# w2's seventh rows fetched mid-run in transfers of three rows, and the rest of w2 in four parts

## The chip, the cores and the metric

One core of a Trainium2 chip runs the whole kernel. The metric is device time in microseconds (us), as the median of timed executions; the kernel before takes 1312.24 us (three runs, 1311.43 to 1312.91).

## The reference

One decoding step for eight tokens (batch 8, model width 512). The normalised input goes into two branches, whose results are added to the input:

```python
xn = layernorm(x)                              # 8 x 512
q = xn @ wq                                    # 32 heads of 128; 8 key/value heads
p = softmax(q k^T * 128**-0.5)                 # 8192 cached keys for each head
a = (p @ v) @ wo                               # wo: 4096 x 512
h = xn @ w1 + b1                               # 1792 wide
m = (h * tanh(softplus(h))) @ w2               # w2: 1792 x 512
return x + a + m
```

All is float32. The cached keys and values are 268 MB each, read once, and outweigh the weights by far: wq and wo are 8.4 MB each, w1 and w2 3.7 MB each.

## The kernel before

The work is cut into 32 units, `j` = 0 to 31: one of four groups of two key/value heads (`m`), with one of eight tokens (`b`). For each unit 8.39 MB of keys (kT) and 8.39 MB of values (v) are fetched, each by one transfer to all 128 partitions. All of them go to one on-chip tile, `kv`, 40960 floats to a partition: v in floats 0 to 16383, kT of even units from 16384, kT of odd units from 24576, so that the two places of kT overlap by half. w1 lies where the first even kT will come (from 16384), and w2 comes from 32768 on at the end. `load_unit` (L137 to L145) issues these transfers on SP's queue.

A unit runs so (loop L549 to L587; in the names of the profile `s` are scores, `e` exponentials, `pt` turned exponentials, `o` and `os` the weighted values):

- `scores`, L314 on TensorE (PE): 32 matmuls of the keys against the masked queries `wk`, in two halves, 64 instructions in the profile. Between the halves the next unit's kT is issued (L558). It overwrites the half that the first half of the scores has read, so SP waits for that half.
- `softmax`, L326 to L346, and the next unit's masked queries, L297 on VectorE (DVE).
- `values` of the unit before, L393: 32 matmuls. Then v of this unit is issued (L572), since its place is free.
- `turn`, L350 to L379: a matmul of `e` against a permutation into `x`, then DVE transposes and sums that make `pt`. Then `merge`, L410.

The program's order is written by hand: each engine does its instructions in the order in which the code calls them, and waits where it must. SP's transfers likewise start in the order of issue. The completion of transfers from SP and from ScalarE's (ACT's) queue is told by eight semaphores, taken in turn; an issue waits for the last transfer that had its semaphore.

In unit 0, before `turn`, `mish` (L418 to L468) makes the second branch's activation: 18 matmuls (L422, L430) into `h`, then a chain of DVE operations in w1's place, and at its end `aT` (L465), the activation turned, 14 groups of eight columns. kT of unit 2 comes to that place, so its issue waits for L465.

Ahead of the loop DVE makes small tables from an identity (`bsel`, `usel` and so on, L162 to L206), then does the layer norm; the first queries are projected from wq in the tile `ws` (L250), which is used four times, last in unit 21, with its masked queries read in unit 23.

After the loop SP issues wo in four parts of 2 MB, and w2 in three parts (L600): of the seven rows of w2 that a partition holds, four, two and one, that is 2, 1 and 0.5 MB. PE does the last `values`, the products with wo (`outputs`, L500, into the bank `a`), the products of w2's first part into the same bank (`down_wide`, L511), and while ACT copies `a` out (L615), the second part's into `h` (`down`, L523); then the copy's rows are summed into `h` (L618), and the third part's products follow. DVE adds the residual `xres` (L627), and SP stores the result. `xres` comes to `ws` in 16 pieces of 1 KB from GpSimd's (POOL's) queue (L544), issued from unit 23 on.

## Time and profile before

| | us |
|---|---|
| median of three runs | 1312.24 |
| the profiled execution | 1313.53 |
| its span in the profile | 1310.3 |
| PE busy | 907.7 |
| DVE busy | 407.4 |
| ACT busy | 41.8 |
| read from HBM: 561 MB, over the span | 428 GB/s |

The span is the time from the first to the last event of the core; some 3 us of the execution lie around it. The profile's stages are read by time from the span's start: the first unit's chain reaches until about 78 us, the units repeat until about 1267 us, and the end with wo and w2 follows.

### The profile page before, as it was taken

How to read it: one execution, taken by the hardware profiler on the slowest of the kernel's cores; microseconds unless marked ns; L12 is line 12 of the kernel's file. 1: busy time of each engine (PE TensorE's matmuls, PEld its weight loads, DVE VectorE, ACT ScalarE, POOL GpSimd, SP SyncE). 2: the span in 40 equal slices, each digit the busy share in tenths (PEclk: the TensorE clock that was granted, in tenths of full speed). 3: DMA queues.
4: the chain of work that ended last, by engine and by line, in shares of the span. 5: the costliest groups of instructions: out<-in, count | busy, mean ns of one | idle time of the engine just before them, and what ended most of it. 6: DMA issues, size and time to landing. Idle time of an engine off the chain costs nothing.

```text
span 1310.3 us, 10389 instructions
## 1 busy us (share of the span) xinstructions
PE 907.7 (69%) x4568; PEld 269.2 (21%) x4568; DVE 407.4 (31%) x881; ACT 41.8 (3%) x96; POOL 10.1 (1%) x24
## 2 busy tenths in 40 slices
PE   4967866768767567777668766687576668657667
PEld 1212221212212112222112212122121112212112
DVE  3363132331333333123331332322233331233330
ACT  1000000000000000000000000000000000000000
POOL 0000000000000000000000000011000000000000
PEclk9979887888888888887798788798887898887788
DMA  9999999999999999999999999999999999999997
GB/s 404 444 427 437 431 433 427 437 440 431 433 431 435 425 441 425 441 426 439 429 433 433 431 437 425 444 421 441 425 437 433 435 429 437 431 436 427 437 417 312
DMA packets 11668, 561.75 MB, mean 429 GB/s; under 512 B 1724, under 2 KB 1888, under 8 KB 2024
## 3 DMA queue, kind: packets, MB, share of 16 engines
q1 hardware_dynamic: 11088, 561.06, 99.2%
q8 instruction: 35, 0.57, 0.2%
q0 software_dynamic: 512, 0.02, 0.0%
q10 hardware_dynamic: 24, 0.02, 0.0%
q14 instruction: 9, 0.07, 0.0%
HBM read 561.03 MB, written 0.07 MB: 428 GB/s over the span
## 4 chain that ended last, share of the span: by engine, by line
DMA 73%; PE 23%; DVE 2%; ACT 0%; issue 0%; SPq 0%; DVEq 0%
DMA kv<-in_v 71%; PE o L393 20%; DMA kv<-in_w 3%; PE s L314 1%; PE h L250 1%; PE h L422 0%; DVE kv L452 0%; DVE tr L363 0%; PE h L523 0%; DVE wk L297 0%; DVE pt L379 0%; DVE y L373 0%; DVE nm L326 0%; ACT L216 0%; DVE ws L270 0%
## 5 line engine op out<-in xcount | busy, mean ns | idle before, releaser
L314 PE MATMUL s<-kv,wk 128*64 128x512 f32 x2048 | 512.9, 665 | 247.5 <-DMA kv<-in_kT 244.8
L393 PE MATMUL o<-kv,pt 128*32 128x512 f32 x2048 | 269.6, 686 | 46.5 <-DMA kv<-in_v 46.5
L314 PEld LDWEIGHTS s<-kv,wk 128*64 128x64 f32 x2048 | 157.5, 154 | 583.1 <-issue 327.3
L326 DVE TENSOR_REDUCE nm<-s 128x1 f32<-128x512 f32 x32 | 22.1, 692 | 547.7 <-PE s L314 547.7
L393 PEld LDWEIGHTS o<-kv,pt 128*32 128x32 f32 x2048 | 70.4, 123 | 219.5 <-issue 178.8
L363 DVE STREAM_TRANSPOSE tr<-x 128x512 f32<-128x512 f32 x128 | 79.8, 681 | 0.1
L401 DVE TENSOR_SCALAR os<-o,isel 128x128 f32<-128x128 f32 x32 | 11.2, 351 | 220.2 <-PE o L393 220.2
L297 DVE TENSOR_TENSOR wk<-qr,mask 128x512 f32<-128x512 f32 x64 | 62.5, 1019 | 5.7 <-ACT qr L286 5.7
L379 DVE SCALAR_TENSOR_TENSOR pt<-tr,gsum,y 64x256 f32<-64x256 f32 x128 | 56.2, 478 | 1.7
L345 ACT ACTIVATE e<-s,nmx 128x512 f32<-128x512 f32 x32 | 22.0, 688 | 1053.1 <-DVE nmx L342 1053.1
L373 DVE SCALAR_TENSOR_TENSOR y<-tr,gsum,y 128x512 f32<-128x512 f32 x64 | 48.4, 756 | 2.3
L350 PE MATMUL x<-e,perm 128*128 128x512 f32 x64 | 36.0, 644 | 0.0
L403 DVE SCALAR_TENSOR_TENSOR os<-o,isel,os 128x128 f32<-128x128 f32 x96 | 33.7, 351 | 3.4
L250 PE MATMUL h<-ws,xn 128*8 128x512 f32 x64 | 31.7, 642 | 0.0
L327 PE MATMUL m<-ident,nm 128*1 128x128 f32 x32 | 8.7, 273 | 29.3 <-DVE nm L326 29.3
L410 PE MATMUL m<-ident,os 128*128 128x128 f32 x32 | 10.3, 323 | 22.2 <-DVE os L403 12.2
L371 DVE TENSOR_SCALAR y<-tr,gsum 128x512 f32<-128x512 f32 x32 | 24.1, 754 | 1.1
L338 PE MATMUL m<-ident,nx 1*128 1x1 f32 x32 | 7.0, 219 | 24.1 <-DVE nx L334 24.1
L346 DVE TENSOR_SCALAR lsum<-rsel,l 128x8 f32<-128x8 f32 x32 | 7.4, 231 | 30.3 <-ACT e L345 30.3
L544 POOL DMA_DIRECT2D ws<-in_x x16 | 8.4, 527 | 901.9 <-PE h L250 870.8
L331 DVE TENSOR_REDUCE nr<-m 1x4 f32<-1x64 f32 x64 | 11.0, 207 | 11.7 <-PE m L327 11.7
L350 PEld LDWEIGHTS x<-e,perm 128*128 128x128 f32 x64 | 9.5, 188 | 23.7 <-issue 21.7
(107 smaller groups left out, 152.7 us busy)
## 6 DMA issues: line engine op xcount, KB each, us to landing
ws<-in_wq SPq DMA_DIRECT2D x4, 2048.0 KB, 34.3
kv<-in_wo SPq DMA_DIRECT2D x4, 2048.0 KB, 24.2
kv<-in_w SPq DMA_DIRECT2D x1, 3584.0 KB, 22.1
kv<-in_w SPq DMA_DIRECT2D x1, 2048.0 KB, 34.7
kv<-in_w SPq DMA_DIRECT2D x1, 1024.0 KB, 36.7
kv<-in_kT SPq DMA_DIRECT2D x32, 29.8
kv<-in_v SPq DMA_DIRECT2D x32, 30.1
kv<-in_w SPq DMA_DIRECT2D x1, 512.0 KB, 37.4
```

What stands on the lines that cost most here:

```text
L250: nc.tensor.matmul(H[:B, :], xn4[:, c, :], w[:, c, d * 512 : (d + 1) * 512], start=(c == 0), stop=(c == CC - 1),)
L297: nc.vector.tensor_mul(w[:, :, d], q[:, :, d].to_broadcast([P, DI, NH * G, REP]), mask[:, d * NH * G : (d + 1) * NH * G] .rearrange("p (o ...
L314: nc.tensor.matmul(S[64 * c : 64 * (c + 1), :], w[:, i].rearrange("p d k h -> p (d k h)"), kk[:, i, c, :], start=(part == 0 and n == 0), s ...
L326: nc.vector.tensor_reduce(nm, S, axis=AX.X, op=ALU.max, negate=True)
L345: nc.scalar.activation(e, S, AF.Exp, bias=nmx, accum_out=l)
L350: nc.tensor.matmul(X, perm, e, start=True, stop=True)
L363: nc.vector.transpose(tr.rearrange("p (l t) c -> p t l c", t=TL)[:, tl], X.rearrange("p (t o q l) -> p t l o q", t=TL, o=1, q=PP)[:, tl].t ...
L371: nc.vector.tensor_scalar(y, kinds[:, 0], gsum[:, 0:1], None, op0=ALU.mult)
L373: nc.vector.scalar_tensor_tensor(y, kinds[:, g], gsum[:, g : g + 1], y, op0=ALU.mult, op1=ALU.add)
L379: nc.vector.scalar_tensor_tensor(pt8[half, c, :, d * REP : (d + 1) * REP], kinds[half, 3, :, c * REP : (c + 1) * REP], gsum[half, 3:4], y[ ...
L393: nc.tensor.matmul(O[Q * q : Q * (q + 1), :], pt8[:, c, TL * l : TL * (l + 1), :].rearrange("p t h -> p (t h)"), vt[:, 512 * n : 512 * (n ...
L403: nc.vector.scalar_tensor_tensor(os, O[:, DH * i : DH * (i + 1)], isel[:, i : i + 1], os, op0=ALU.mult, op1=ALU.add)
```

## The change

The last of the seven rows of w2 that each partition holds (128 rows of 4 KB, 0.5 MB) is no longer fetched at the end. Seventeen transfers on ACT's queue bring these rows in units 24 to 31 into `ws`, which is free then: eight of 12 rows (three partitions, four rows to each), eight of three rows (one to a partition), and one of the eight rows that remain. Partitions p, p + 4 and p + 8 take part in one transfer, from 0 to 11 and 32 to 43. Since a row no longer lies on the partition of its activation, `deal_early` in unit 0, after `mish`, deals the last two column groups of `aT` to the new partitions: a masked copy on DVE, a matmul with a selection table `esel`, and a copy on ACT into `aE`. The tables `esel` and `kmask` are made ahead of the layer norm by nine more DVE operations. `early_products` multiplies: eight matmuls in unit 29, and four after the last `values`, all into bank `a`, whose accumulation they now begin.

The rest of w2, six rows to a partition, comes in four parts of two, two, one and one rows. `down_wide` takes the first two, `down` the others. `xres` moves to floats 39936 and on of `kv`, and comes in four pieces of eight rows, issued after the loop.

The diff:

```diff
--- before.py
+++ after.py
@@ -64,7 +64,11 @@
 
 LOAD_Q, MAKE_Q, SPREAD_Q = 4, 5, 7
 
-CUTS = tuple((g, lo, lo + 2) for g in range(G) for lo in range(0, B, 2))
+LEAD, LS, LK = 3, 4, 4
+SPAN, SLOTS = LEAD * LS, LK + 2
+SLOT4 = (LK + 1) * 2 * SPAN
+EARLY_AT = {24: (0, 2), 25: (2, 4), 26: (4, 6), 27: (6, 8), 29: (8, 11), 30: (11, 14), 31: (14, 17)}
+PRODUCE_AT = {29: (0, LK)}
 
 
 @with_exitstack
@@ -124,7 +128,10 @@
     qsel = const.tile([P, P], F32, name="qsel")
     oW = const.tile([P, NP, WOR, 2, B], F32, name="oW")
     qr = const.tile([P, DI, H2 * B], F32, name="qr")
-    xres = ws[:, :P]
+    xres = kv[:, W2_AT + 7168 : W2_AT + 7168 + P]
+    esel = const.tile([P, 2 * Q], F32, name="esel")
+    kmask = const.tile([P, SLOTS], F32, name="kmask")
+    aE = const.tile([2 * Q, SLOTS, 2, B], F32, name="aE")
     oT = const.tile([P, 2, H2, B], F32, name="oT")
     aT = const.tile([P, 2 * W2R, B], F32, name="aT")
     pt8 = const.tile([P, HALF, PL * TL, H2], F32, name="pt8")
@@ -165,6 +172,21 @@
             perm.rearrange("p (d k c h) -> p d k c h", d=2, c=2, h=REP)[:, d],
             ident.rearrange("p (c d k h) -> p d k c h", c=2, d=2, h=REP)[:, d],
         )
+    nc.vector.memset(esel, 0.0)
+    first = ident[:, : LK * 2 * SPAN].rearrange("p (u s k e) -> p u e s k", u=2, s=LS, k=LK)
+    second = ident[:, LK * 2 * SPAN : SLOT4].rearrange("p (u s e) -> p u e s", u=2, s=LS)
+    for u in range(2):
+        to = esel[:, Q * u : Q * u + SPAN].rearrange("p (e s) -> p e s", e=LEAD)
+        nc.vector.reduce_sum(to, first[:, u], axis=AX.X)
+        nc.vector.tensor_add(to, to, second[:, u])
+    nc.vector.tensor_add(esel[:, : P - SLOT4], esel[:, : P - SLOT4], ident[:, SLOT4:])
+    nc.vector.reduce_sum(
+        kmask[:, :LK],
+        ident[:, : LK * 2 * SPAN].rearrange("p (x k e) -> p k x e", k=LK, e=LEAD),
+        axis=AX.XY,
+    )
+    nc.vector.reduce_sum(kmask[:, LK : LK + 1], ident[:, LK * 2 * SPAN : SLOT4], axis=AX.X)
+    nc.vector.reduce_sum(kmask[:, LK + 1 :], ident[:, SLOT4:], axis=AX.X)
     nc.vector.reduce_sum(
         gsum, ident.rearrange("p (x g q) -> p g x q", g=4, q=PP), axis=AX.XY
     )
@@ -468,6 +490,24 @@
             )
 
 
+    def deal_early():
+
+        last = work.tile([P, 512], F32, name="e")[:, : SLOTS * 2 * B]
+        nc.vector.tensor_mul(
+            last.rearrange("p (k c) -> p k c", k=SLOTS),
+            aT[:, 2 * W2R - 2 :]
+            .rearrange("p (o e) b -> p o (e b)", o=1)
+            .to_broadcast([P, SLOTS, 2 * B]),
+            kmask.rearrange("p (k o) -> p k o", o=1).to_broadcast([P, SLOTS, 2 * B]),
+        )
+        nc.tensor.matmul(
+            M[: 2 * Q, 192 : 192 + SLOTS * 2 * B], esel, last, start=True, stop=True
+        )
+        nc.scalar.copy(
+            aE.rearrange("p k e b -> p (k e b)"),
+            M[: 2 * Q, 192 : 192 + SLOTS * 2 * B],
+        )
+
     TURN = {}
 
     def turn_masked(m):
@@ -501,7 +541,7 @@
                     A[Q * i : Q * i + B, :],
                     oW[:, m, i, h, :],
                     w[:, i, h],
-                    start=(m == 0 and h == 0),
+                    start=False,
                     stop=False,
                 )
 
@@ -513,7 +553,7 @@
                 aT[:, j, :],
                 w[:, at : at + D],
                 start=False,
-                stop=(j >= 2 * hi - G),
+                stop=(j >= 2 * parts[2][0] - G),
             )
 
     def down(lo, hi, w, first):
@@ -525,7 +565,7 @@
                     aT[:, j, :],
                     w[:, at : at + P],
                     start=(first and j == 2 * lo),
-                    stop=(j == 2 * W2R - 1),
+                    stop=(j == 2 * W2R - 3),
                 )
 
 
@@ -539,11 +579,39 @@
     spread()
     key_weights(0)
 
-    def residual(g, lo, hi):
-
-        nc.gpsimd.dma_start(
-            xres[Q * g + lo : Q * g + hi, :], x[lo:hi, g * P : (g + 1) * P]
-        )
+    late_rows = w2.rearrange("j p f -> (j p) f").rearrange("(q i) f -> q i f", i=W2R)[:, W2R - 1]
+
+    def early(n):
+
+        turn, at = divmod(n, 2 * LS)
+        u, s = divmod(at, LS)
+        p = Q * u + s
+        rows = slice(p, p + (LEAD - 1) * LS + 1, LS)
+        if turn == 0:
+            q = at * LK * LEAD
+            nc.scalar.dma_start(
+                ws[rows, : LK * BW].rearrange("e (k f) -> e k f", k=LK),
+                late_rows[q : q + LK * LEAD].rearrange("(k e) f -> e k f", e=LEAD),
+            )
+        elif turn == 1:
+            q = LK * 2 * SPAN + at * LEAD
+            nc.scalar.dma_start(ws[rows, :BW], late_rows[q : q + LEAD])
+        else:
+            nc.scalar.dma_start(ws[: P - SLOT4, BW : 2 * BW], late_rows[SLOT4:])
+
+    def early_products(lo, hi):
+
+        for n in range(2 * lo, 2 * hi):
+            k, e = divmod(n, 2)
+            at = (k - lo) * BW + e * D
+            rows = Q + SPAN if k <= LK else P - SLOT4
+            nc.tensor.matmul(
+                A[Q * (n % G) : Q * (n % G) + B, :],
+                aE[:rows, k, e],
+                ws[:rows, at : at + D],
+                start=(n < G),
+                stop=False,
+            )
 
     v_t = {}
     for j in range(UNITS):
@@ -573,10 +641,14 @@
             if spreads:
                 spread()
                 key_weights(j + 1)
-        for cut in CUTS[2 * (j - 23) : 2 * (j - 22)] if j >= 23 else ():
-            residual(*cut)
+        if j in PRODUCE_AT:
+            early_products(*PRODUCE_AT[j])
+        if j in EARLY_AT:
+            for n in range(*EARLY_AT[j]):
+                early(n)
         if j == 0:
             mish(w1_t, b1_sb, kv[:, W1_AT : W1_AT + 6 * FG])
+            deal_early()
         if more and b == LOAD_Q:
             load_q(j // B + 1)
         if more and b == MAKE_Q:
@@ -587,6 +659,8 @@
             merge(j - 1, os)
 
 
+    for g in range(G):
+        nc.gpsimd.dma_start(xres[Q * g : Q * g + B], x[:, g * P : (g + 1) * P])
     w_o = [kv[:, 4096 * m : 4096 * (m + 1)] for m in range(NP)]
     for m in range(NP):
         nc.sync.dma_start(
@@ -597,13 +671,14 @@
         )
     w2_rows = w2.rearrange("j p f -> (j p) f").rearrange("(q i) f -> q (i f)", i=W2R)
     w2_t = []
-    parts = ((0, 4), (4, 6), (6, 7))
+    parts = ((0, 2), (2, 4), (4, 5), (5, 6))
     for lo, hi in parts:
         t = kv[:, W2_AT + lo * BW : W2_AT + hi * BW]
         nc.sync.dma_start(t, w2_rows[:, lo * BW : hi * BW])
         w2_t.append(t)
 
     os = values(UNITS - 1, v_t.pop(UNITS - 1))
+    early_products(LK, SLOTS)
     for m in range(NP - 1):
         outputs(m, w_o[m])
     merge(UNITS - 1, os)
@@ -611,9 +686,10 @@
     turn_rows(NP - 1)
     outputs(NP - 1, w_o[NP - 1])
     down_wide(*parts[0], w2_t[0])
+    down_wide(*parts[1], w2_t[1])
     a_sb = work.tile([P, 512], F32, name="e")
     nc.scalar.copy(a_sb, A)
-    down(*parts[1], w2_t[1], True)
+    down(*parts[2], w2_t[2], True)
     for g in range(G):
         nc.tensor.matmul(
             H[Q * g : Q * g + B, :P],
@@ -622,7 +698,7 @@
             start=False,
             stop=False,
         )
-    down(*parts[2], w2_t[2], False)
+    down(*parts[3], w2_t[3], False)
     res = work.tile([P, DH], F32, name="os", bufs=1)
     nc.vector.tensor_add(res, H[:, :P], xres)
     nc.sync.dma_start(out, res)
```

Where it moves PE's instructions in units 0 and 1 (`h` is `mish`'s bank, `m` the bank for small turns, `x` that of `turn`, `s` the scores), before:

```order
L430 MATMUL h<-kv 16x448 [waits DMAHW2_49]
L430 MATMUL h<-kv 16x448
L350 MATMUL x<-e,perm 128x512 [waits Activation_49]
L314 MATMUL s<-kv,wk 64x512 [waits DMAHW5_49,DVE_49]
L314 MATMUL s<-kv,wk 64x512 x31
```

and in the change, where L372 is the old L350, and L336 the old L314:

```order
L452 MATMUL h<-kv 16x448 [waits DMAHW2_49]
L452 MATMUL h<-kv 16x448
L503 MATMUL m<-e,esel 64x96 [waits DVE_49]
L372 MATMUL x<-e,perm 128x512 [waits Activation_49]
L336 MATMUL s<-kv,wk 64x512 [waits DMAHW5_49]
L336 MATMUL s<-kv,wk 64x512 x31
```

The matmul of `deal_early`, which reads the end of `mish`'s DVE chain, stands between `mish`'s matmuls and the turn of unit 0, and ahead of the scores of unit 1.

SP's queue at the same place, in the change (L148 is the old L141): the waits of the third kT are the same as before.

```order
L148 DMA kv<-in_kT 128x16384
L148 DMA kv<-in_v 128x16384 [waits DMAHW3_49,PE_49]
L148 DMA kv<-in_kT 128x16384 [waits DMAHW4_49,DMAHW2_49,DMAHW5_49,DVE_49,PE_49]
L148 DMA kv<-in_v 128x16384 [waits DMAHW6_49,PE_49]
L148 DMA kv<-in_kT 128x16384 [waits DMAHW7_49,DMAHW1_49,PE_49]
```

Nothing moved here; the third kT waits for DVE (`aT`) and for PE (the first half of the scores of unit 1).

PE at the end, in the change, behind the products with wo (L551 is the old L511, L563 the old L523, L694 the old L618):

```order
L551 MATMUL a<-kv,aT 8x512 [waits DMAHW4_49]
L551 MATMUL a<-kv,aT 8x512 x3
L551 MATMUL a<-kv,aT 8x512 [waits DMAHW5_49]
L551 MATMUL a<-kv,aT 8x512 x3
L563 MATMUL h<-kv,aT 8x128 [waits DMAHW6_49]
L563 MATMUL h<-kv,aT 8x128 x7
L694 MATMUL h<-e,bsel 8x128 [waits Activation_49]
L694 MATMUL h<-e,bsel 8x128 x3
L563 MATMUL h<-kv,aT 8x128 [waits DMAHW7_49]
L563 MATMUL h<-kv,aT 8x128 x7
```

Before, eight matmuls of L511 came after one part's landing, and 16 of L523 after the second's; now there are four, four and eight, each after a part of its own. The last eight are as before.

## The prediction

> **What bounds the kernel now.** The page's chain first, then the stages by time.
>
> ```profile
> DMA 73%; PE 23%; DVE 2%; ACT 0%; issue 0%; SPq 0%; DVEq 0%
> 40.00:200.00 160.00, 118.02 (x610) 34.84 (x605) 60.02 (x123) 5.75 (x12) 0.00 (x0) 0.87 1.00 434
> 945.00:1200.00 255.00, 171.44 (x876) 51.17 (x878) 82.43 (x177) 7.03 (x18) 0.00 (x0) 0.83 1.00 433
> 1285.00:1298.00 13.00, 9.28 (x83) 2.47 (x79) 2.83 (x9) 0.41 (x2) 0.00 (x0) 1.00 1.00 420
> 1298.00:1303.00 5.00, 2.17 (x24) 0.34 (x16) 0.00 (x0) 0.00 (x0) 0.00 (x0) 1.00 0.55 233
> ```
>
> The first line is the chain that ended last, by engine. The others are stretches of the span; their last three columns are the clock granted to PE, the busy share of the sixteen DMA engines, and GB/s. From 40 us on the share is 1.00 at 433 or 434 GB/s: transfers are the bound, and time in which the queue is empty is lost for good, since nothing later runs below its rate. Behind 1298 us the share falls to 0.55, some nine of sixteen engines: seven have finished, the others run until w2's last part has landed, at 1305.8 (below). The rows don't say which are the early ones.
>
> What feeds the queue is SP's issues, which wait for compute to free a place:
>
> ```profile
> SPq L141 <- PE s L314: 298.7, 31, 20.3
> 48.22 0.33 SPq L141 DMA_DIRECT2D kv<-in_v  x1
> kv<-in_v SPq DMA_DIRECT2D x1, 27.9
> 69.25 0.33 SPq L141 DMA_DIRECT2D kv<-in_kT  x1
> kv<-in_kT SPq DMA_DIRECT2D x1, 26.3
> 86.86 0.33 SPq L141 DMA_DIRECT2D kv<-in_v  x1
> 68.74 0.44 DVE L465 COPY aT<-kv 64x112 f32<-64x112 f32 x2
> ```
>
> The first row sums SP's waits for the scores: 31 of them. Then the issues of v of unit 0, kT of unit 2 and v of unit 1, with us to landing behind the first two. That v lands at 48.22 + 27.9 = 76.1; kT lands at 69.25 + 26.3 = 95.6, 19.5 us later, just its own transfer (8.39 MB at 434 GB/s is 19.3 us). So kT was waiting in the queue, issued in time. It goes out at 69.25 because `aT` was finished at 69.18, the last row; its other condition, the first half of unit 1's scores, had been met.
>
> **The added matmul in unit 0, and what stands behind it.** PE works in order. The matmul of `deal_early` needs `aT`, and the turn of unit 0 and all scores of unit 1 now stand behind it.
>
> ```profile
> 57.12 1.13 PE L350 MATMUL x<-e,perm 128*128 128x512 f32 x2
> 58.18 13.95 PE L314 MATMUL s<-kv,wk 128*64 128x512 f32 x64
> L171 DVE TENSOR_REDUCE mask<-ident 128x16 f32<-128x128 f32 x1 | 0.3, 276 | 0.0
> L220 DVE TENSOR_SCALAR st<-st 8x1 f32<-8x1 f32 x1 | 0.1, 142 | 0.0
> L475 DVE TENSOR_TENSOR oT<-oT,rt 128x64 f32<-128x64 f32 x4 | 1.1, 264 | 0.0
> L477 DVE TENSOR_TENSOR e<-oT,usel 128x256 f32<-128x256 f32 x4 | 1.7, 425 | 0.1
> 1267.88 0.33 PE L352 MATMUL m<-lsum,ones 128*128 128x64 f32 x2
> ```
>
> Before, the scores began at 58.18, 11 us ahead of `aT`. Now:
>
> - Nine small DVE operations stand ahead of the layer norm, whose chain leads to `aT`. A reduction of the identity takes 276 ns, started some 0.2 us apart; the shortest operation 142 ns. Nine cost 1.3 to 2.5 us; I take 1.6. `aT` is done at 70.8.
> - The masked copy, 128x96, lies between 264 ns (128x64) and 425 ns (128x256): 0.3. The matmul: like the pair of L352, 0.33, and 0.1 for the handover. Then the turn of unit 0, 1.06 until the scores follow (57.12 to 58.18). They begin at 70.8 + 0.3 + 0.43 + 1.06 = 72.6.
>
> kT of unit 2 then waits for their first half.
>
> ```profile
> 95.63 15.37 PE L314 MATMUL s<-kv,wk 128*64 128x512 f32 x64 [6.87 <-DMA kv<-in_kT]
> 104.17 0.33 SPq L141 DMA_DIRECT2D kv<-in_kT  x1
> 211.93 16.94 PE L314 MATMUL s<-kv,wk 128*64 128x512 f32 x64 [10.44 <-DMA kv<-in_kT]
> 222.05 0.33 SPq L141 DMA_DIRECT2D kv<-in_kT  x1
> 59.00:72.00 13.00, 13.00 (x62) 4.17 (x58) 12.39 (x20) 0.19 (x1) 0.00 (x0) 1.00 1.07 464
> 134.30:139.00 4.70, 4.67 (x12) 1.48 (x14) 0.00 (x0) 0.00 (x0) 0.00 (x0) 0.50 1.00 432
> ```
>
> A half took 8.5 us in unit 2 (95.63, kT issued at 104.17) and 10.1 in unit 5 (211.93 to 222.05), and 7.0 at 58.18, where PE had been kept busy (half of 13.95). The clock explains it: 1.00 in 59 to 72 us, 0.50 when PE started again at 134.3. Now PE will have been idle for some 14 us, but the turn runs first: I take 8.7, with bounds 7.0 and 10.1. kT is issued at 81.3, 12.05 us later than before.
>
> The Trainium skill ("TensorE: Matmul & The Clock Gate", What's actually happening) has a half clock after an idle window of about 3.4 us, and the full one after about as long a busy one. The 0.50 agrees; by that rule the half would take about 7.9 us, and the result be 0.8 us lower than below.
>
> How much of the 12.05 the queue covers:
>
> ```profile
> out<-os SPq DMA_DIRECT2D x1, 64.0 KB, 1.6
> ws<-in_wq SPq DMA_DIRECT2D x1, 2048.0 KB, 7.8
> ```
>
> A transfer that finds the queue empty needs more than its bytes: the output, 64 KB, lands in 1.6 us, 0.15 of it bytes; the first wq, 2.1 MB, in 7.8, 4.8 of it bytes. That is 1.45 to 3.0 us over. A lone kT lands 20.8 to 22.3 us from its issue, against 26.3 measured: the cover is 4.0 to 5.5 us. With 5.0 the stall is 12.05 - 5.0 = 7.05. A landing is told by the last engine, and those that finished the v before it wait longer; I take 7.6 us, with bounds 4.5 (half of 7.0 us, and all cover) and 10.3 (2.5 us of DVE, half of 10.1, least cover).
>
> What is late next is v of unit 1, which needs the weighted values of unit 0: scores until 72.6 + 15.7, then 2.0 of softmax (111.00, the end of the scores at 95.63, to 113.03), then values.
>
> ```profile
> 112.81 0.22 PE L338 MATMUL m<-ident,nx 1*128 1x1 f32 x1 [0.75 <-DVE nx L334]
> 78.06 8.73 PE L393 MATMUL o<-kv,pt 128*32 128x512 f32 x64
> ```
>
> It is issued at 99.1 instead of 86.86, alone would land by 120.4, but kT, landing at about 102.9, lets it land at 122.2 at the earliest. Hidden; a second stall is at most 1 us. From there each unit repeats with its old distances, so all later stages shift alike.
>
> **The end.** Per engine 32 of 224 KB of w2 go, at 434/16 = 27.1 GB/s: 1.21 us.
>
> ```profile
> 1267.42 1.38 SPq L603 DMA_DIRECT2D kv<-in_w  x3
> kv<-in_w SPq DMA_DIRECT2D x1, 512.0 KB, 37.4
> 1302.14 2.39 PE L511 MATMUL a<-kv,aT 128*8 128x512 f32 x16 [2.83 <-DMA kv<-in_w]
> 1304.61 1.90 PE L523 MATMUL h<-kv,aT 128*8 128x128 f32 x32
> 1304.63 0.59 ACT L615 COPY e<-a 128x512 f32<-128x512 f32 x1 [7.28 <-PE a L511]
> 1306.28 0.65 PE L618 MATMUL h<-e,bsel 128*8 128x128 f32 x8
> 1306.70 0.68 PE L523 MATMUL h<-kv,aT 128*8 128x128 f32 x16
> ```
>
> In the old times: w2's last part landed at 1268.4 + 37.4 = 1305.8; now the last lands at 1304.6, the third 1.2 earlier, the second at 1302.1, as the old first, and the first at 1299.7. The old chain ran from the second part's landing (1304.61) through 16 matmuls of L523, L618 and the last eight to 1307.38. The new one: half of L511's work from 1302.14, 1.2, then the copy of `a`, 0.6 and its handover, to 1304.0; eight matmuls of L523 from 1303.4, 0.95, to 1304.35; L618 with the copy there, to 1304.8; the last eight with their part landed, 0.68, to 1305.4. That is 2.0 us less; at least the bytes' 1.2, at most 2.3, if the last eight start at the landing with the faster clock.
>
> **Costed at nothing**, each with its cover:
>
> ```profile
> 868.00:945.00 77.00, 54.92 (x265) 16.02 (x257) 22.42 (x47) 1.93 (x4) 8.36 (x16) 0.87 0.99 427
> 1292.36 1.90 PE L500 MATMUL a<-kv,oW 128*8 128x512 f32 x16 [1.54 <-DMA kv<-in_wo]
> 1238.87 15.48 PE L314 MATMUL s<-kv,wk 128*64 128x512 f32 x64 [9.88 <-DMA kv<-in_kT]
> 1277.78 9.61 PE L393 MATMUL o<-kv,pt 128*32 128x512 f32 x64 [8.37 <-DMA kv<-in_v]
> ```
>
> - Interleaved small transfers: 16 residual pieces ran in 868 to 945 us, at 427 instead of 433 GB/s, 1.1 us in all. They go, four come back, and 17 on ACT's queue join: -0.8 to +1.1, taken as 0.
> - ACT's issues wait in unit 29 for the early products, and otherwise for transfers of about two units before. Behind them stands an exponential a unit later. Eight early products, like 16 instructions of L500 (1.90), fit into PE's wait for the next kT, 6.9 to 10.4 us in the rows of L314; the last four, half of that, into the 1.54 us before wo's third part.
> - w2's last part now waits for a semaphore of the last v, for which PE waits until 1277.78, 25 us before the part is needed. `xres` waits for the last scores, done at 1254.35, and then has 50 us.
>
> **Sum.** +7.6 - 2.0 = +5.6 us against the profiled 1313.53 (span 1310.3): 1319.1. That execution lies 1.3 above the median, so the median goes from 1312.24 to 1317.8.
>
> **Rivals.**
>
> *The queue covers the delay*, so only the end's gain shows: 1312.24 - 2.0 = 1310.2. It decides if kT of unit 2 is issued by 69.25 + 5 = 74.3, which needs the scores to begin by 66 us. Against it stand the order on PE and `aT` at 69.18; for it only a wait shorter than I read it, or much more cover than two small transfers show.
>
> *The three-row transfers burden engines that are late.* Each of three engines would take 160 KB more in place of 32 KB: 128 KB at 27.1 GB/s, +4.8 us. Seven engines end about 5 us early (0.55 from 1298 on), and on these it costs nothing; on any of the nine late ones the end comes 4.8 us later: 1317.8 + 4.8 = 1322.6. The partitions chosen don't tell which engines these are.
>
> The Trainium skill ("DMA: Bandwidth & Descriptors", Why a DMA increments its semaphore by 16 and not by 1) says that a transfer runs on the largest number of engines up to 16 that divides its slowest dimension, from the lowest engine up. By it all sixteen three-row transfers fall on the same three engines; no row here shows whether these are early.
>
> *The change only gains more at the end* than 2.6 us, without the stall, is part of the first rival.
>
> **Chances and range.** Forecast 0.74, with its own range 1314.4 to 1322; covered delay 0.13; late engines 0.13. A difference below 0.2% (2.6 us) can't be told from none. Slower by more: 0.74 x 0.95 + 0.13 = 0.83; within: most of the first rival and the low end, 0.11; faster: 0.06. The range 1314.0 to 1322.8 leaves out the first rival and a few of a hundred at the ends.
>
> **What would show it.** Right: the scores of unit 1 begin near 72.6, kT of unit 2 is issued near 81, and the DMA share falls well under 1 between 74 and 83 us; the last part lands about 6 us later than now, and PE is done within 1 us of it. Wrong: kT issued before 75 us; a DMA share that stays low for 10 us at the end on three engines; or ACT's issues delaying an exponential in units 24 to 31.

## The result, and the profile after

| | median of runs (us) | runs | profiled execution: time, span (us) |
|---|---|---|---|
| before | 1312.58 (1311.23 to 1313.65) | 6 | 1313.53, 1310.3 |
| after | 1319.47 (1318.22 to 1320.35) | 6 | 1320.3, 1318.4 |

The ratio is 1.0053, with a 95% interval of 1.004 to 1.0066: slower, by 6.9 us, where +5.6 had been forecast, to 1317.8. The two spans differ by 8.1 us and the times of the same two executions by 6.8, because 3.2 us of the profiled execution of before lie outside its span; in that of after it is 1.9.

First the stretches of time (the last three columns: PE's granted clock, the share of the sixteen DMA engines, GB/s), of before:

```profile
60.00:200.00 140.00, 99.57 (x524) 29.52 (x521) 54.41 (x111) 3.11 (x8) 0.00 (x0) 0.85 1.00 430
```

and of after:

```profile
60.00:200.00 140.00, 95.10 (x467) 28.53 (x467) 51.84 (x104) 3.14 (x8) 0.00 (x0) 0.83 0.93 401
72.00:74.00 2.00, 2.00 (x4) 0.50 (x6) 0.09 (x1) 0.14 (x1) 0.00 (x0) 0.50 0.30 131
74.00:82.00 8.00, 8.00 (x34) 2.42 (x34) 6.43 (x11) 0.00 (x0) 0.00 (x0) 0.85 0.00 0
1308.00:1312.00 4.00, 2.29 (x20) 0.23 (x12) 0.00 (x0) 0.00 (x0) 0.00 (x0) 1.00 0.74 308
```

Over 60 to 200 us the rate fell from 430 to 401 GB/s. That is 29 x 140 us / 430 = 9.4 us of transfers, and nearly all of it lies in one hole: from about 73 us to 82 no byte moved. The last row is the other place where the kernels differ: in the last microseconds of the transfers the share is about 0.75, where before it was 0.55 (1298 to 1303 us, shown in the prediction): as much as twelve engines of sixteen instead of nine.

The hole has its cause in the order of instructions on PE (the timeline of after, PE with VectorE's and SP's rows by time; brackets hold the idle time before an instruction and what ended it):

```profile
70.50 0.43 DVE L487 COPY aT<-kv 64x112 f32<-64x112 f32 x2
70.97 0.26 DVE L496 TENSOR_TENSOR e<-aT,kmask 128x96 f32<-128x96 f32 x1
71.28 0.58 PE L503 MATMUL m<-e,esel 128*64 128x96 f32 x2 [12.29 <-DVE e L496]
71.80 2.07 PE L372 MATMUL x<-e,perm 128*128 128x512 f32 x2
73.80 15.21 PE L336 MATMUL s<-kv,wk 128*64 128x512 f32 x64
82.19 0.33 SPq L148 DMA_DIRECT2D kv<-in_kT  x1
98.21 0.33 SPq L148 DMA_DIRECT2D kv<-in_v  x1
105.31 16.51 PE L336 MATMUL s<-kv,wk 128*64 128x512 f32 x64 [5.20 <-DMA kv<-in_kT]
```

`aT` is finished at 70.93 (L487), the masked copy at 71.23, and L503, for which PE had been idle for 12.29 us, runs at 71.28. The turn of unit 0 follows, 2.07 us for the pair instead of 1.13, then the scores of unit 1 from 73.80 (before: 58.18). kT of unit 2 goes out at 82.19 instead of 69.25. It finds an empty queue and lands 23.1 us later, at 105.3, when the scores that waited for it begin; before, it landed at 95.6. So the stall is 9.7 us.

The end, before (one row, the output's issue) and after:

```profile
1307.78 0.35 SPq L628 DMA_DIRECT2D out<-os  x1
```

```profile
1309.65 1.04 PE L551 MATMUL a<-kv,aT 128*8 128x512 f32 x8 [0.40 <-DMA kv<-in_w]
1312.12 1.04 PE L551 MATMUL a<-kv,aT 128*8 128x512 f32 x8 [1.42 <-DMA kv<-in_w]
1313.36 0.62 PE L563 MATMUL h<-kv,aT 128*8 128x128 f32 x16 [0.20 <-DMA kv<-in_w]
1314.61 0.62 PE L563 MATMUL h<-kv,aT 128*8 128x128 f32 x16 [0.28 <-DMA kv<-in_w]
1315.62 0.35 SPq L704 DMA_DIRECT2D out<-os  x1
```

The output is issued 7.84 us later than before: of the 9.7 us, 1.9 come back. Each of w2's four parts is awaited by PE (L551 twice, L563 twice), and the last eight matmuls start at their landing.

### The profile page after: what moved, and what is told of

It reads as the page before. It is cut to its first block, busy times and chain, and to the rows that moved or that the text cites. A ratio compares the mean times of both kernels' runs of the same rounds, so it can differ in the third digit from the quotient of the medians.

```text
span 1318.4 us, 10431 instructions
## 1 busy us (share of the span) xinstructions
PE 906.5 (69%) x4578; PEld 267.8 (20%) x4578; DVE 408.0 (31%) x891; ACT 42.0 (3%) x97; POOL 3.9 (0%) x12
## 4 chain that ended last, share of the span: by engine, by line
DMA 72%; PE 25%; DVE 2%; issue 0%; ACT 0%
DMA kv<-in_kT 68%; PE s L336 23%; DMA kv<-in_v 2%; DMA kv<-in_w 2%; PE h L272 1%; PE h L444 0%; DVE kv L474 0%; PE x L372 0%; DVE wk L319 0%; PE y L301 0%; ACT L238 0%; PE x L301 0%; DVE ws L292 0%; ACT e L280 0%; DVE kv L250 0%
## 5 line engine op out<-in xcount | busy, mean ns | idle before, releaser
L336 PE MATMUL s<-kv,wk 128*64 128x512 f32 x2048 | 516.7, 669 | 249.5 <-DMA kv<-in_kT 246.9
L415 PE MATMUL o<-kv,pt 128*32 128x512 f32 x2048 | 261.4, 669 | 46.2 <-DMA kv<-in_v 46.2
L336 PEld LDWEIGHTS s<-kv,wk 128*64 128x64 f32 x2048 | 158.2, 154 | 590.2 <-issue 331.9
L367 ACT ACTIVATE e<-s,nmx 128x512 f32<-128x512 f32 x32 | 22.0, 687 | 1051.2 <-DVE nmx L364 1051.2
L372 PE MATMUL x<-e,perm 128*128 128x512 f32 x64 | 36.9, 659 | 0.0
L372 PEld LDWEIGHTS x<-e,perm 128*128 128x128 f32 x64 | 9.7, 191 | 23.2 <-issue 21.2
```

Of the source, the lines that this page charges most:

```text
L336: nc.tensor.matmul(S[64 * c : 64 * (c + 1), :], w[:, i].rearrange("p d k h -> p (d k h)"), kk[:, i, c, :], start=(part == 0 and n == 0), s ...
L367: nc.scalar.activation(e, S, AF.Exp, bias=nmx, accum_out=l)
L372: nc.tensor.matmul(X, perm, e, start=True, stop=True)
L415: nc.tensor.matmul(O[Q * q : Q * (q + 1), :], pt8[:, c, TL * l : TL * (l + 1), :].rearrange("p t h -> p (t h)"), vt[:, 512 * n : 512 * (n ...
```

## The experiments

Theories: (A) the stall alone makes the kernel slower, and how long it is depends on when kT of unit 2 and v of unit 1 are issued; the rest of the change gains 1 to 2 us. (B) The three-row transfers or their issues on ScalarE cost time. (C) Something else of the change does: the tables, the residual, the parts. All ratios are to the kernel before, run on the same chip.

### The step moved to where nothing waits for it

`deal_early` is called at the end of unit 2, where `aT` has long been finished; all else is the change's.

```diff
         if j == 0:
             mish(w1_t, b1_sb, kv[:, W1_AT : W1_AT + 6 * FG])
-            deal_early()
...
+        if j == 2:
+            deal_early()
```

> The change, with deal_early moved from unit 0 to the end of unit 2, where PE waits for keys anyway. Stall theory (all that the change loses comes from the deal's matmul standing ahead of unit 1's scores): kT of unit 2 is issued near 71 us again, the DMA share stays at 1 between 73 and 85 us, and the time is 1.5 to 2.5 us below the kernel before (about 1310.5 us). Rival (the transfers of three rows and their three engines cost something too): 0 to 5 us above the kernel before.

Measured: 1310.88 us (1310.54 to 1311.63, 11 runs) against 1311.89, ratio 0.9995, interval 0.9986 to 1.0003.

```profile
60.00:200.00 140.00, 100.01 (x519) 30.00 (x519) 54.60 (x111) 3.35 (x9) 0.00 (x0) 0.85 1.00 431
69.64 0.33 SPq L148 DMA_DIRECT2D kv<-in_kT  x1
```

The hole is gone, kT of unit 2 goes out at 69.64, and with that the whole slowdown: against its own runs of before the change is at +6.9 us, this kernel at -1.0. Tables, early transfers, early products, residual and parts together cost nothing that can be measured; a small cost that the gain at the end makes up is not excluded. What they gain, 1.0 us where 1.5 to 2.5 had been expected, can't be told from nothing.

### The step alone

The kernel before, with the tables and `deal_early` in unit 0, whose result nothing uses; w2, the residual and the end are as before. The lines of the tables and of `deal_early` itself, as in the change, are left out here.

```diff
         if j == 0:
             mish(w1_t, b1_sb, kv[:, W1_AT : W1_AT + 6 * FG])
+            deal_early()
```

> The kernel before, with the nine table operations and deal_early in unit 0 added, its result unused; nothing else of the change. Stall theory: kT of unit 2 lands near 105 us, as in the change, and the time is 9 to 10 us above the kernel before. Rival (the stall is partly made up later, or part of the loss is the transfers'): 4 to 7 us above.

Measured: 1321.38 us (1320.31 to 1323.29, 5 runs), ratio 1.0076, interval 1.0063 to 1.009: +9.5.

```profile
60.00:200.00 140.00, 96.58 (x468) 28.79 (x468) 52.61 (x107) 2.57 (x7) 0.00 (x0) 0.83 0.94 404
80.86 0.33 SPq L148 DMA_DIRECT2D kv<-in_kT  x1
```

With the one before it, this is the change taken apart: this step without the rest costs 9.5 us, the rest without this step nothing that can be measured. The two add up to 8.5 us, and the change has 6.9; the intervals (8.3 to 11.8, -1.8 to 0.4, and 5.3 to 8.7) allow for that.

### The whole step behind the turn, or between the halves

Two kernels that should have shortened the stall. In the first `deal_early` stands behind the turn of unit 0; in the second, between the first and the second half of unit 1's scores, so that the half that kT of unit 2 waits for is ahead of it.

```diff
+++ both
-            deal_early()
+++ behind the turn
         turn(j, late)
+        if j == 0:
+            deal_early()
+++ between the halves
             k_t[j + 1] = load_unit(kT, j + 1, K_AT[(j + 1) % 2])
+        if j == 1:
+            deal_early()
         scores(j, k, j % 2 == 0, 1)
```

> The change, with deal_early behind the turn of unit 0: the turn's matmul no longer waits, but unit 1's scores still do. Stall theory: the scores begin near 72 us instead of 73.8, kT of unit 2 goes out near 80.5, and the time is 1 to 2.5 us below the change (about 1317.5 us). Rival (it is the turn and the DVE work behind it that came late): the time falls back to that of the kernel before or below.

> The change, with deal_early between the two halves of unit 1's scores. Stall theory (only the first half releases kT's place): kT of unit 2 goes out near 71 us, as soon as the activation is turned; v of unit 1 is late instead, near 92 to 95 us against 86.9 before, which costs 0 to 2 us; time 2 us below to 1 us above the kernel before. Rival (any matmul waiting for the activation ahead of the end of unit 1's scores costs the same): 5 us or more above the kernel before.

Measured: behind the turn 1325.4 us (1324.25 to 1326.07, 4 runs), ratio 1.0104, interval 1.009 to 1.0118; between the halves 1314.85 (1314.36 to 1317.64, 6 runs), ratio 1.0029, interval 1.0017 to 1.004; before, 1311.89. The first is 5.9 us above the change where 1 to 2.5 below had been expected, the second 3.0 above before where 2 below to 1 above had been. The first's rows:

```profile
60.00:200.00 140.00, 90.95 (x457) 32.10 (x459) 51.25 (x102) 2.57 (x7) 0.00 (x0) 0.82 0.90 389
76.56 0.26 DVE L496 TENSOR_TENSOR e<-aT,kmask 128x96 f32<-128x96 f32 x1
86.11 0.33 SPq L148 DMA_DIRECT2D kv<-in_kT  x1
```

and those of the other:

```profile
60.00:200.00 140.00, 97.03 (x475) 31.29 (x475) 53.41 (x110) 3.82 (x10) 0.00 (x0) 0.83 0.96 413
77.54 0.42 PE L503 MATMUL m<-e,esel 128*64 128x96 f32 x1 [10.99 <-DVE e L496]
98.25 0.33 SPq L148 DMA_DIRECT2D kv<-in_v  x1
```

What I had missed is the second engine on which the step has a place. Its masked copy runs on VectorE, which does its instructions in the order of the program too, and moving the call put it behind VectorE's part of the turn, which ran from 69.80 to 76.55. So the copy ran at 76.56, in the change at 70.97, and PE waited that much longer. So kT was issued at 86.11 and the stall grew. Between the halves kT was issued on time (70.50), but the second half waited until 77.54 [10.99 us idle], v of unit 1 went out at 98.25 instead of 86.77, after the queue had run dry (no byte moved from 94 to 98 us), and the stall came there. Both miss their numbers. Read after the fact, both fit theory A: what is late moves from kT to v, and the time follows. The next two kernels test that reading.

### The step split, VectorE's part where it was

The same two places again, but only for the matmul and the copy behind it; the masked copy stays directly behind `mish`.

```diff
-            deal_early()
+            dealt = deal_early()   # comment added: now ends behind the masked copy
+++ behind the turn
         turn(j, late)
+        if j == 0:
+            deal_rows(dealt)       # comment added: matmul and ScalarE's copy
+++ between the halves
+        if j == 1:
+            deal_rows(dealt)
         scores(j, k, j % 2 == 0, 1)
```

> The change with the masked copy of aT (VectorE) where it was, right after mish, and only its TensorE product and ScalarE copy moved behind the turn of unit 0. So the turn is back ahead of the wait for aT (it ends near 58 us, as before), while VectorE's order is the change's. The theory (what counts is when kT of unit 2 is issued): the scores of unit 1 begin at 71.9 instead of 73.8, the issue comes at 80.3 to 81.4 instead of 82.19, and the run loses what the issue gains: 0.8 to 1.9 below the change, 1317.6 to 1318.7. A rival, in which the 13.5 of the kernel that moved the whole step behind the turn came from TensorE's order and not from VectorE's, has this one at 1325 too. A second rival, in which the issue of kT is not what sets the end, has it level with the change, 1319.5.

> The masked copy right after mish, and its TensorE product and ScalarE copy between the two halves of unit 1's scores. The theory: kT of unit 2 is issued on time (70.5) and lands without a gap; the second half waits for aT and runs from 71.9 to 81, the values end near 90.5, and v of unit 1 is issued at 92 to 93, about when the queue ran dry in the kernel that had the whole step there (share 0.10 from 92 on): a stall of 0 to 1, so 0 to 1.2 above the kernel with the step in unit 2, 1310.9 to 1312.1. The rival, in which any wait of TensorE for aT ahead of unit 1's softmax costs the run the same whatever is issued, has it near the 1314.9 of the kernel that had the whole step there.

Measured: behind the turn 1318.9 us (1318.09 to 1319.19, 5 runs), ratio 1.0049, interval 1.0036 to 1.0063; between the halves 1311.27 (1310.52 to 1313.44, 11 runs), ratio 0.9995, interval 0.9986 to 1.0004; before, 1312.21.

```profile
60.00:200.00 140.00, 93.91 (x475) 32.84 (x479) 54.02 (x111) 3.34 (x9) 0.00 (x0) 0.84 0.96 411
57.69 1.13 PE L372 MATMUL x<-e,perm 128*128 128x512 f32 x2
70.06 0.42 PE L507 MATMUL m<-e,esel 128*64 128x96 f32 x1 [11.24 <-DVE e L496]
79.23 0.33 SPq L148 DMA_DIRECT2D kv<-in_kT  x1
```

```profile
60.00:200.00 140.00, 104.57 (x531) 33.18 (x527) 55.04 (x111) 3.85 (x10) 0.00 (x0) 0.84 1.00 428
70.81 0.42 PE L507 MATMUL m<-e,esel 128*64 128x96 f32 x1 [4.22 <-DVE e L496]
91.52 0.33 SPq L148 DMA_DIRECT2D kv<-in_v  x1
1305.58 0.62 PE L567 MATMUL h<-kv,aT 128*8 128x128 f32 x16 [0.27 <-DMA kv<-in_w]
```

Between the halves the expectation held: PE still idles for `aT` [4.22 us ahead of L507], the scores still end 8.5 us later than before (80.63 instead of 72.13), and it costs nothing that can be measured, since kT (70.54) and v (91.52) are issued before the queue is dry. A wait on PE in itself has no price here. Behind the turn the kernel is 6.5 us below the one with the whole step there, so VectorE's order did make that miss. Against the change it gains 0.2 to 0.6 us (against their own runs of before, by the medians) where 0.8 to 1.9 were expected, too little to be told from nothing. So this kernel alone doesn't exclude the second rival of its expectation, that the issue of kT isn't what sets the end; the series below does. Its kT was issued 3.0 us earlier than the change's, but 1.2 of these come from `aT`, finished at 69.72 in this profiled execution and at 70.93 in the change's. That time varies from one profiled execution to the next, as is told below, under the prediction's points.

The five kernels and the change are one series. The transfers lost in 60 to 200 us follow from the rate, (431 - GB/s) x 140 / 431, and stand beside the span of the profiled execution, less that of the first kernel, and the median's distance from its own runs of before, less the same of the first kernel (-1.0):

| step | kT of unit 2, v of unit 1 issued | GB/s | lost (us) | span | median |
|---|---|---|---|---|---|
| at the end of unit 2 | 69.64, 86.77 | 431 | 0 | 0 | 0 |
| matmul between the halves | 70.54, 91.52 | 428 | 1.0 | -0.2 | +0.1 |
| whole step between the halves | 70.50, 98.25 | 413 | 5.8 | +5.5 | +4.0 |
| matmul behind the turn | 79.23, 95.25 | 411 | 6.5 | +6.7 | +7.7 |
| the change | 82.19, 98.21 | 401 | 9.7 | +8.8 | +7.9 |
| whole step behind the turn | 86.11, 102.12 | 389 | 13.6 | +12.8 | +14.5 |

From 0 to 13.6 us the span follows what the queue lost within about 1.2 us, the median within about 1.8. Theory A stands. (The matmul behind the turn and the change differ by 3.2 us in what their queues lost, by 2.1 in their spans, and hardly in their medians: the one profiled is the shortest run but one of its kernel, 1318.09 to 1319.19, the other all but the longest of its own. The whole step between the halves was likewise profiled in a long run, 1316.85, 2.0 above its median.)

### The early transfers: once by sixteen engines, or twice

In the first of these, w2's seventh rows come by one transfer of 128 rows in unit 24 and are multiplied in unit 29 by two matmuls with the last two column groups of `aT`, with no dealing at all; w2's rest comes in the change's four parts. The second is the kernel with the step in unit 2, with each transfer of twelve rows issued twice on the spot. The third has them twice too, but the first time in the units 16 to 19.

```diff
+++ sixteen engines
+        if j == 24:
+            nc.scalar.dma_start(ws[:, :BW], late_rows)
+        if j == 29:
+            early_products()
+++ twice on the spot
-            nc.scalar.dma_start(
+            for _ in range(2):
+                nc.scalar.dma_start(
+++ twice, once earlier
+ONCE_MORE = {16: (0, 2), 17: (2, 4), 18: (4, 6), 19: (6, 8)}
...
+        if j in ONCE_MORE:
+            for n in range(*ONCE_MORE[j]):
+                early(n)
```

> The change without dealing: the seventh rows come mid-run by one transfer to all 128 partitions in unit 24, so all sixteen engines carry them, as at the end before; two products with them in unit 29, no tables, no deal_early; the four parts as in the change. Theory (the end gains 1.2 us by bytes put on engines that are early, and 0.8 us by a shorter chain of matmuls): 0.5 to 1.1 us below the kernel before, and about 1.2 us above the change with a late deal. Rival (what counts is only that the rows come earlier): the same 2 us below as with the late deal.

> The change with deal_early in unit 2 and each of the eight transfers of twelve rows made twice: 393 KB more, or 131 KB and 4.8 us for each of three engines. Theory (three rows mean three engines, which the change has brought near the late ones): the three engines end last, and the time is 2.5 to 4.8 us above that of the same kernel with the rows once. Rival (the bytes spread over all engines, or the three have much room left): 0 to 1 us above.

> The kernel with the step in unit 2, and the eight transfers of twelve rows issued a second time, two in each of the units 16 to 19 (into the query tile, idle there), so that no ninth transfer waits for a semaphore soon after. The theory of the early engines: the eight transfers go to three engines of the seven that are about 6 us ahead, and cost each some 4.2; once they fit, twice they put these three about 2.4 behind the nine late ones, so the end moves by 1.5 to 3 and the time is 1312.4 to 1313.9. If bytes on all sixteen counted, 8 transfers of 48 KB at the 433 GB/s of the middle of the run cost 0.9: 1311.8. If small transfers cost the run nothing at all, it stays at 1310.9. If ScalarE's waits for the transfers matter here as they did when the eight were doubled on the spot, the time is over 1316 and the trace shows ScalarE's queue blocked.

Measured: by sixteen engines 1311.54 us (1311.35 to 1312.35, 11 runs), ratio 0.9997, interval 0.9988 to 1.0006, not to be told from before (0.5 to 1.1 below had been expected) or from the kernel with the step in unit 2. So whether it buys anything to bring these rows by three engines, with the dealing that this needs, instead of by all sixteen, is not shown. Twice on the spot 1328.47 (1327.6 to 1328.92, 4 runs), ratio 1.0126, interval 1.0113 to 1.014. Twice, once earlier, 1316.05 (1315.81 to 1316.78, 7 runs), ratio 1.0029, interval 1.0018 to 1.004.

The second failed as an experiment, for a reason of its own (ScalarE's timeline, its issues marked ACTq):

```profile
985.15 0.85 ACTq L593 DMA_DIRECT2D ws<-in_w  x1
1000.31 27.86 ACTq L593 DMA_DIRECT2D ws<-in_w  x3
1028.27 0.69 ACT L367 ACTIVATE e<-s,nmx 128x512 f32<-128x512 f32 x1 [42.45 <-DMA ws<-in_w]
1062.95 0.20 ACT L531 COPY oW<-m 32x64 f32<-32x64 f32 x1 [33.90 <-DMA ws<-in_w]
1060.00:1070.00 10.00, 6.30 (x23) 2.14 (x25) 6.62 (x12) 0.41 (x2) 0.00 (x0) 0.66 0.10 38
```

The copy of a transfer writes the same rows, so its issue waited until the first had landed, 15 us after 985.15, and again within the 27.86 us of the next three. Behind them on ScalarE stood the exponential of unit 25 (L367), which ran at 1028.27 instead of 1023.47 in the kernel with the step in unit 2, and later ScalarE's copies for the output projection (L531), at 1062.95 instead of 1034.71. PE idled 29.28 us for these copies with the next scores behind them, SP's next kT waited for the scores until 1072.59 (1052.45), and the queue ran dry: 0.10 from 1060 to 1070 us. So it says nothing on engines; it shows what the change avoids by having no early transfer wait long on ScalarE: in the kernel with the step in unit 2 each issue of twelve rows takes 0.7 to 0.9 us.

The third has no such wait: its issues of twelve rows take 0.7 to 0.9 us each. The rows are SP's issues of kT in the units 25 and 28 and two windows at the end, of this kernel and then of the one that has the transfers once:

```profile
1014.23 0.33 SPq L149 DMA_DIRECT2D kv<-in_kT  x1
1135.65 0.33 SPq L149 DMA_DIRECT2D kv<-in_kT  x1
1304.00:1306.00 2.00, 2.00 (x20) 0.23 (x12) 0.00 (x0) 0.00 (x0) 0.00 (x0) 1.00 0.23 94
1306.00:1308.00 2.00, 0.58 (x8) 0.12 (x8) 0.00 (x0) 0.00 (x0) 0.00 (x0) 1.00 0.19 78
```

```profile
1014.32 0.33 SPq L148 DMA_DIRECT2D kv<-in_kT  x1
1130.42 0.33 SPq L148 DMA_DIRECT2D kv<-in_kT  x1
1302.00:1304.00 2.00, 1.42 (x12) 0.28 (x16) 0.00 (x0) 0.00 (x0) 0.00 (x0) 0.74 0.50 203
1304.00:1306.00 2.00, 2.00 (x44) 1.17 (x36) 0.00 (x0) 0.59 (x1) 0.00 (x0) 0.50 0.06 16
```

With the first eight transfers done long ago the two kernels are level, within 0.1 us at 1014. During and after the second eight this one's issues of kT are 2.3 to 5.2 us behind (1054 to 1212 us; 5.2 in the rows shown), its span ends 4.3 us later, and its median, each against its own runs of before, is 4.9 higher. At its end the share is 0.23 and 0.19 for 4 us; three engines of sixteen are 0.19. In the other kernel the share falls from 0.50 to 0.06 within as long. So three engines take all of these transfers. The share shows the first set too: from 1298 to 1302 us it is 0.77 and 0.73 in the kernel that has it once by three engines, 0.61 and 0.55 in the one that has it by sixteen. A set is 8 x 48 KB / 3 = 128 KB for each, 4.8 us at the prediction's 27.1 GB/s: the second set costs all or nearly all of its bytes, the first nothing that can be measured. Spread over sixteen engines the same bytes would have been 0.9 us, by the expectation's sum. These three were early by about the 5 us that the prediction read from the share of 0.55, and one set uses that up. My expectation of 1.5 to 3.0 came from a lead of 6 and a set of 4.2, both a little off.

The Trainium skill ("DMA: Bandwidth & Descriptors", Why a DMA increments its semaphore by 16 and not by 1) lets a transfer use the largest number of engines up to 16 that divides its slowest dimension, here three, beginning with the lowest. The 0.19 agrees with the number; which engines they are no row shows.

### The other parts, alone

The kernel before with w2 in five parts at the end, and the kernel before with the residual loaded in four pieces behind the last unit.

```diff
+++ the parts
-    parts = ((0, 4), (4, 6), (6, 7))
+    parts = ((0, 2), (2, 4), (4, 5), (5, 6), (6, 7))
+++ the residual
-        for cut in CUTS[2 * (j - 23) : 2 * (j - 22)] if j >= 23 else ():
-            residual(*cut)
...
+    for g in range(G):
+        nc.gpsimd.dma_start(xres[Q * g : Q * g + B], x[:, g * P : (g + 1) * P])
```

> The kernel before with w2 in five parts of two, two, one, one and one rows, all at the end; nothing else. The bytes stay; only the chain of matmuls behind the last landings is shorter. Theory: 0.3 to 1 us below the kernel before. Rival (the parts alone give the whole gain at the end): 2 us below.

> The kernel before with the residual in four pieces behind the loop instead of sixteen within it; nothing else. The 868 to 945 us stretch ran at 427 instead of 433 GB/s, 1.1 us. Theory (the pieces cost nothing that shows): within 0.5 us of the kernel before. Rival (they cost what the stretch shows): 0.8 to 1.2 us below.

Measured: 1311.85 us (11 runs), ratio 1.0, interval 0.9991 to 1.0009, and 1311.75 (11 runs), ratio 0.9999, interval 0.999 to 1.0008. Neither does anything that can be measured; for the parts 0.3 to 1 us of gain had been expected. Theory C falls, by these two for its parts and by the kernel with the step in unit 2 for all of them together, and B with it for the transfers as the change issues them.

## Why the prediction was right, point by point

| step | predicted | measured |
|---|---|---|
| `aT` finished | 70.8 | 70.93, by luck (below) |
| masked copy, matmul, handover | 0.73 us | 0.83 (70.97 to 71.80) |
| turn of unit 0, until the scores | 1.06 us | 2.00 (71.80 to 73.80) |
| scores of unit 1 begin | 72.6 | 73.80 |
| first half, until kT of unit 2 is issued | 8.7 us, 81.3 | 8.39 us, 82.19 |
| kT lands, alone in the queue | 20.8 to 22.3 us after its issue | 23.1 |
| stall | 7.6 us (4.5 to 10.3) | 9.7 |
| v of unit 1 issued | 99.1, hidden | 98.21, hidden |
| end's gain | 2.0 us (1.2 to 2.3) | 1.9 in the pair of traces; 1.0 with the stall removed, not to be told from nothing |
| small transfers, issues on ScalarE | 0 | none measurable, by the kernel with the step in unit 2 |
| sum | +5.6 | +6.9 by the medians; +7.8 in the pair of traces |

**The mechanism** was the predicted one, place by place. The two kernels that split it, and the series, show it; it isn't only read off the trace. The 0.9 us between the medians and the traces lies outside the spans, as told with the result.

**That `aT` came when forecast is luck.** The nine operations cost about what was priced: VectorE starts the layer norm 1.27 us later (1.6 forecast). The forecast carried this straight to `aT`. These are VectorE's start and the scores of unit 0, before and after:

```profile
6.08 0.67 DVE L209 TENSOR_REDUCE st<-kv 8x1 f32<-8x512 f32 x1
32.53 15.65 PE L314 MATMUL s<-kv,wk 128*64 128x512 f32 x64 [2.64 <-DVE wk L297]
```

```profile
7.35 0.67 DVE L231 TENSOR_REDUCE st<-kv 8x1 f32<-8x512 f32 x1
33.30 16.67 PE L336 MATMUL s<-kv,wk 128*64 128x512 f32 x64 [2.63 <-DVE wk L319]
```

But in between PE made up for the 1.27 us and lost them again. Its first eight products with wq took 5.04 us instead of 6.49, and the spreading of the queries behind them (L301, the old L279) began at 27.71, earlier than before (27.90). From 28 to 33 us its granted clock was then 0.56 in the change's profiled execution and 1.00 in that of before; the scores began 0.77 us later and took 1.02 longer, and `aT` was 1.75 us late. Profiled executions vary in this: in the nine kernels here that have the nine operations `aT` was finished between 69.57 and 71.19, in the four that don't, before among them, between 68.48 and 70.01. The means, 70.17 and 69.16, lie 1.0 us apart, so a term of about that size is there, but that one execution came within 0.13 us of the forecast says little.

**The stall was sized 2.1 us too small**, by two terms. The turn was priced at a warm PE, by a row of before in which PE came out of long work (57.12); after 12.29 us of idling it ran at a clock of 0.50 and took twice as long. The prediction had said that PE would have idled, applied it to the half and not to the turn ahead of it: 0.9 us. The other is the cover, 1.2 us of it: a kT that finds the queue empty landed 3.8 us over its 19.3 us of bytes, not 1.45 to 3.0 as read from a 64 KB and a 2 MB transfer. The cover was 26.3 - 23.1 = 3.2 us, below its bounds of 4.0 to 5.5. With 82.19 - 69.25 = 12.94 us of delay that gives 9.7. The Trainium skill ("DMA: Bandwidth & Descriptors", Anatomy of one DMA) has a fixed part of about 2.0 us for a transfer issued by GpSimd; an estimate from that is 21.3 us for kT at this rate. kT, issued by SP, took 1.8 us more, and the measurement decides.

**The half** took 8.39 us where 8.7 was taken and the rule of the Trainium skill would have had 7.9 ("TensorE: Matmul & The Clock Gate", What's actually happening); the truth lies between.

**The end** gained less than forecast once the stall is removed. These are its rows in the kernel with the step in unit 2:

```profile
1302.58 1.58 PE L551 MATMUL a<-kv,aT 128*8 128x512 f32 x8 [1.42 <-DMA kv<-in_w]
1305.29 1.08 PE L563 MATMUL h<-kv,aT 128*8 128x128 f32 x16
1306.75 0.35 SPq L705 DMA_DIRECT2D out<-os  x1
```

The second part is there at 1302.58 (forecast 1302.1). From there to the end of the last eight it takes 3.79 us at a clock of 0.50 (the window above), where the change, at 1.00, takes 3.11. The forecast had 3.3 us for that chain. So of the 1.0 us that is missing about half is the clock, and half the second part's later landing. In the kernel with the matmul between the halves the clock stayed up, and the last part landed at 1305.6, a microsecond after the forecast 1304.6, as much as its queue had lost in the series. So some 0.5 us of the forecast gain hang on the clock that PE happens to have in the last 5 us, and what is left, about 1 us of 1312, none of these comparisons can tell from nothing.

**The rivals.** That the queue covers the delay was false for kT at 82.19 and true for v at 91.52: the cover is real but only some 3 us long. That the three-row transfers burden late engines was false: the three are early ones. With as many transfers of twelve rows again it would have been true, at 4.3 to 4.9 us, near the 4.8 that it was priced at.

**The baseline.** The profiled execution of before lay 1.3 us above its median; the prediction took the median, and had to: what was high in it was for the most part the time outside the span, 3.2 us.

## What to carry to other kernels

When transfers bound a kernel, price an instruction that is put into an in-order engine's program by what it delays at the queue: find the next DMA issue behind it, its distance to the moment at which the queue runs dry, and take the difference. The same step cost 0, 4, 8 or 14.5 us here, by its place and what stood behind it, and a step that spans two engines has a place on both, each to be looked up. A delay early in such a chain needn't arrive at its end: look for the waits in between that take it up. Sixteen engines that end unevenly were a reserve here: transfers of three partitions' rows were free on engines that were early, until the lead was used up, and then cost about their full bytes.

## What the runs showed of the hardware that was not expected

- A transfer of 8.39 MB that finds the queue empty lands 23.1 us after its issue (23.0 to 23.1 in three more of these kernels), 3.8 over its bytes at 434 GB/s; the transfers of 64 KB and 2 MB that the prediction went by show 1.45 and 3.0.
- The sixteen engines finish some 5 us apart after 1300 us of transfers (the share of 0.55 from 1298 us on), and three of the early ones took one set of 4.8 us each at no cost that can be measured. What makes them early stays open.
- How long PE's clock stays at half when PE starts again varies. In the six kernels of these experiments, the change among them, in which PE started again for this step between 70 and 78 us, it was 3.8 to 5.2 us. The windows from 74 to 76 us, of the kernel with the matmul behind the turn, where PE had started at 70.06 after 11.24 us of idling, and of the one with it between the halves, started at 70.81 after 4.22 us:

```profile
74.00:76.00 2.00, 2.00 (x12) 1.24 (x10) 1.85 (x5) 0.00 (x0) 0.00 (x0) 1.00 0.00 0
```

```profile
74.00:76.00 2.00, 2.00 (x6) 0.92 (x4) 1.86 (x3) 0.00 (x0) 0.00 (x0) 0.50 1.14 492
```

The third number from the right is the clock: 1.00 less than 4 us after the start in the first, still 0.50 after 5.2 us in the second. The Trainium skill ("TensorE: Matmul & The Clock Gate", What's actually happening) has full rate after a wholly busy window of about 3.4 us, and says that the windows run freely; an estimate from that is 3.4 to 6.8 us, and all six lie within. The prediction's sentence on that rule had taken 3.4 for it.
